# A conditioned convolution and gated-MLP block on one Trainium2 core: the MLP's transposes go to two PSUM tiles, GpSimd joins in normalizing and modulating, and the written-out order is new

## The chip, the cores and the metric

The kernel runs on one core of one Trainium2 chip. The core has a matrix engine (TensorE, "PE" in the profile; its weight loads are "PEld"), three elementwise engines (VectorE "DVE", ScalarE "ACT", GpSimd "POOL") and SyncE ("SP"), which here only starts DMA transfers. ACT starts some transfers too, in its own instruction stream. Every engine executes its instructions in the order in which they were written; between engines there are semaphores. The metric is the device time of one execution in microseconds (us), smaller is better, as the median of several executions.

## What is computed

The reference, cut to what matters (S = 2048 positions, D = 640 channels, 864 gate columns):

```
def A(q, k, v, shift_k, ssm_k, ssm_D):
    k_shift = sum over t of k_pad[:, t:t+S] * shift_k[:, 3-t]        # 4 taps
    kv = k_shift * v
    y = irfft(rfft(kv padded to 2S) * rfft(ssm_k padded to 2S))[:S]  # long convolution
    return q * (y + kv * ssm_D)

def B(x, w_in, w_sp, b_sp, w_out):
    z = gelu(x @ w_in)
    z1 = z[..., :864]
    z2 = layernorm(z[..., 864:])
    g = w_sp @ z2 + b_sp[:, None]
    return (z1 * g) @ w_out

sa, ca, ga, sb, cb, gb = split6(silu(c) @ w_mod)
x = A_q
h = layernorm(x) * (1 + ca) + sa
x = x + ga * A(h, A_k, A_v, ...)
h = layernorm(x) * (1 + cb) + sb
x = x + gb * B(h, ...)
```

All arrays are bf16.

## The kernel before

The 2048 positions are 16 tiles n = 0..15 of 128 rows, in four groups g = 0..3 of four tiles. The 640 channels are five units u = 0..4 of 128. All work up to the mixing matrix `w_sp` is put into a plan: `op(engines, kind, fn, r, w, new, n)` records an operation, the engines that may run it (P TensorE, A ScalarE, D VectorE, G GpSimd, S SyncE), what it reads and writes. The order in which all 1032 operations are issued, and the engine of each, stands written out in `ORDER` (line 40): `A147` means operation 147 on ScalarE. `Plan.run` (L112) only checks that an entry's engine is allowed and its inputs come earlier, and issues. An engine therefore works through its own entries strictly in that order; one that waits holds up everything behind it on its engine.

The stages, with the kinds of operations (the string in `op`) that the text uses:

- **Tables and the short convolution, to about 27 us.** `f1c` (L291) and `msin` (L340) are sines on ACT, after `silut` (L747), the warm-up that makes ACT load its first function table; `f1m` (L292), `msub`, `turns` build tables on DVE. `load_X` (L372) brings ssm_k in as tile X; for u = 0 it comes in two halves of 256 KB, and `addD` (L392) adds ssm_D to it on DVE. `ld1` (L738) loads three small vectors: shift_k (`skr`), ssm_D (`Dr`), c (`cr`). `turn1` turns them on PE, `skc` copies shift_k's columns, `diag` (L530, L528 on ACT) makes diagonal matrices of them, `taps` (L546) convolves k on PE and `tv` (L545) multiplies by v on DVE. `kvw` (L551) writes kv to a scratch in HBM, and `load_X` reads it back as XU0..XU4 in the layout for the transform.
- **The long convolution, about 27 to 121 us.** Per unit: stage 1 of the transform of ssm_k and of kv (`s1` on PE, `s1c` copies on ACT or DVE), stage 2 (`fwd` on PE; `khc` copies the kernel's spectrum on ACT), the product of the spectra (`prod`, L454, DVE), its sum into W (`csum`, L468, POOL or DVE), the inverse (`inv` on PE, `zc` copies to Z on ACT or DVE), a DMA transpose of Z to ZT (`zt`, L675), the last stage (`y` on PE, `ym`, L668, on DVE) and the residual (`res`, L688, DVE or POOL). In between run the first layernorm: statistics `ln1`, `rstd1` on POOL, normalizing `xn` (L598 on ACT, L600 otherwise, 128x640 a tile), and the modulation vectors: `ldw` (L610) loads a sixth of w_mod (800 KB) into the one buffer `wm`, `modr` multiplies; `ghm` (L651) applies them in two passes on POOL or DVE.
- **The turn into the MLP, about 121 to 140 us.** Unit 4 is turned on PE (`zfl`, L709; copies `zk`), `yl` is its last stage, `yml` (L730), `res` and the statistics `ln2` (L694), `ag2` (L813), `rstd2` (L184, L185 on POOL), `nmr2` (L817) follow. `zx` normalizes a tile of 128x640 (L827 on ACT, L829 otherwise). For group 0, in two pieces p of two tiles, `hfl` transposes on PE (L841) and `hmod` (L851 on ACT, L853 on DVE) multiplies by 1 + cb and adds sb while it copies from PSUM. For the groups 1 to 3 one DMA transpose a group (`turn`, L871) does the transposing and `hmod2` (L877 on ACT, L879 otherwise, 128x512) modulates in place.
- **The first MLP product, about 133.5 to 193.5 us.** `zz` is five matmuls of 128x432; 64 of them fill PE. Each is followed by `gelu` (L902, ACT), those of z2 by statistics (`stz`, `agz`, `rstdz`, `nmrz`) and `zn`, the normalization of 128x864 (L923 on ACT, L925 on DVE). `gelut` (L776) is a gelu of one column that makes ACT load the gelu table; before, it stands at the very end of ACT's entries.
- **Mixing and projection, 193.5 us to the end** (L964, L985), written as plain loops that the change does not touch.

`fill` operations (L931) are dummy matmuls on PE, `FILLS` gives how many each has. Tiles come from rings of buffers: `SLOTS` names how many buffers a tag has (PSUM tags s1 1, of two banks; sm, pu, pz 2 each, of one bank); a tile's first writer waits until the buffer's last tile is done with. Where two engines read the same PSUM tile, the framework lets them do so only one after the other: an instruction of one engine waits on a semaphore for the last instruction of the other. Transfers signal through eight semaphores that are handed out in turn, so a transfer waits until the one eight places before it, whoever issued it, has landed. 

Of the kernel before, what the change touches and what calls it, by code (L numbers as in the profile page):

```python
# [15 lines left out]
P = 128  # L16
# [8 lines left out]
NU = 5  # L25
# [8 lines left out]
FILLS = (4, 5, 1, 4, 3, )  # L34
# [6 lines left out]
D0 D100 D13 D14 A1 D15 G5 A2 A82 G101 D102 D103 S19 S21 D115 D116 A4 A16 D17 D6 D104 P1027 P7 A10 A23 P1028 P8 S83 A11  # L41
D86 A106 D109 P24 D110 P1029 P145 A105 A118 A117 A111 A147 D25 A146 D87 P148 A149 S20 A150 D121 D122 S523 D18 D119 P26
P151 S22 D27 S88 D153 P154 D155 A123 A124 G125 A120 P30 P28 A112 D31 G113 D114 D29 A152 A156 P165 A166 P163 A164 D127
A33 P139 D140 G126 P161 S32 A162 D90 G107 P133 P171 A172 P142 S34 D134 G135 P227 A228 P169 A170 D108 P136 G36 P157
A158 D143 G144 P229 A230 P167 D527 D528 G48 D529 D530 P37 S35 D38 A137 S84 A168 P159 P231 A160 P41 A232 D42 S3 P173
A175 D174 P176 D177 A178 G141 P39 D40 S85 P179 D181 S524 P182 A180 A183 A184 P43 D44 A531 A532 P185 D186 P233 G60 P9
A12 A533 P201 S46 S47 D202 P195 D196 P191 D192 G187 A234 P55 D56 P217 D218 A534 G188 P53 S45 G138 P189 A190 P211 D212
G197 G198 P199 A200 D54 P205 D206 G213 G214 D535 P49 P221 G207 G208 D222 P203 S526 A542 P51 S89 P251 D252 A204 P237
A543 P209 D52 S525 D538 A238 D210 P247 A248 D50 P257 A258 P215 D216 P241 P245 G130 G131 G72 A242 A246 P253 P193 D539
G536 D537 S565 P566 P249 A254 A544 A250 P568 P255 A256 D194 P235 D540 S91 D93 D549 D541 A236 P239 A240 S57 G223 G224  # L50
P225 P301 D302 A567 P243 A244 P259 D260 P219 D220 P303 P291 D292 S570 S58 A545 D546 P265 D266 A304 D550 A569 A226 P573
S92 P307 A308 P571 G261 G262 P263 A264 S59 P275 D276 P305 A306 P293 A294 G547 D548 D574 A557 P285 D286 G287 P325 A326
D558 D572 P267 D559 P309 A310 D551 D552 G707 D288 P269 D270 P327 A328 P65 D66 A561 G649 P315 A316 P329 A330 D562 P63
D64 D591 P295 P313 S575 P576 D577 A268 S94 D96 D296 A314 A128 D129 G271 P331 P289 A332 A560 S70 P61 G272 D62 P273 A274
G612 P375 A376 P333 D563 A290 G297 D298 P319 D553 A320 A554 P67 D595 D334 P377 A378 P299 D592 G596 P578 P323 A324 A555
A556 D68 D564 D579 D597 P349 D350 P73 P379 A380 G335 G336 G616 P343 A300 D344 D593 P77 G655 P337 P311 P321 A312 D598
S71 D78 A322 P381 D74 A382 A338 P369 D370 G594 P277 A278 D650 S599 P600 D601 G345 G346 P317 P279 D280 G371 A318 G372
P79 P347 A348 G618 P365 P351 A352 D80 G281 D282 P602 P383 G614 A384 S69 D366 S95 P399 A400 P359 G613 P387 A388 P373
P401 G656 A402 D603 P604 D653 P283 A284 A374 D360 P353 D605 P606 P403 A404 D361 G362 P395 D354 D607 P75 S97 D99 A396
D672 P397 A398 G676 G355 G356 P405 A406 G617 P385 D673 P339 D340 A386 P367 A368 S580 P449 G619 A450 D76 P413 D414 G615  # L60
P407 P363 P453 A454 G608 D408 S620 G409 A364 D410 G713 P341 P393 A394 P621 A342 P451 G654 P389 D622 G674 P623 D624
P439 P411 A390 A452 D440 P357 A358 P625 D626 P391 A392 P427 D428 A412 P455 G708 P627 P417 G429 S81 S98 A456 P415 A416
P473 A474 D418 G419 G420 P433 P457 A458 D430 D434 P431 D651 P479 G435 A480 P471 A472 D628 P443 D444 P475 A476 D629
P421 A432 P423 D424 P461 A462 P477 A478 D632 S657 P581 A582 G436 G652 P658 D659 G445 G446 P463 P481 D482 A464 A422
P437 A438 G675 G670 G671 P660 D661 P467 A468 G677 D633 P447 A448 P497 D498 G483 G484 P441 P662 D663 P517 D518 D630
G634 A442 P425 A426 P465 A466 P664 D665 G519 P459 A460 P507 P485 D508 P501 G520 D502 A486 P499 S583 A500 P469 A470
G609 P521 D637 A522 P513 P487 P584 D666 G509 G510 P511 A512 G503 A585 G504 D514 G714 S678 D488 P491 D492 G493 P515
A516 D494 P505 A506 P679 D680 P489 A490 G709 D636 S586 P681 D682 D635 P495 P683 D684 A496 P719 G610 G711 D720 P721
A722 P685 D686 G702 D687 D691 P717 P715 D716 A718 D689 P587 A588 D688 S753 D631 P723 D724 S754 D725 D726 P746 D727
D755 G667 D756 D728 D729 D747 G757 D758 P732 P589 D731 D690 D759 A760 D730 D768 D767 D692 P1030 P1031 P761 D762 D766  # L70
A764 A765 D763 P739 P789 P779 D693 G769 D770 A772 A771 G710 D733 D734 D736 D695 D738 D735 D638 A780 G712 P786 A787
A790 D696 P773 A775 D829 D737 G639 D831 A777 A778 P809 A810 G644 D694 D832 P811 A812 D830 P813 A814 D776 D774 D697
G668 D700 G833 D834 D835 A838 A837 D836 D669 S839 D740 D642 D741 D742 D744 D641 D703 D705 P815 A816 D745 D611 D645
A590 P793 A794 D748 D752 D743 P782 A783 P796 P819 A820 D841 A797 D798 P817 A818 P807 A808 D844 D842 A843 D640 D701
D643 D698 D898 D699 A840 P803 A804 D784 P800 A801 P821 A822 D895 D896 D897 G899 P845 A846 D847 D900 D901 D903 P862
A863 P885 P848 A886 D904 D802 A849 D850 A902 S905 P873 A874 P875 A876 P852 A853 P869 A870 D647 D805 D854 P866 A867
D648 P879 D750 A880 P855 A856 A910 D871 P859 A860 P881 A908 D788 D704 P883 A884 D646 A882 D751 P887 D962 D907 P877
A878 D909 D906 P951 P925 D706 D964 A952 P911 A888 A926 P932 P914 D749 D961 A933 P945 D963 G965 D966 D967 A912 A915
A946 D970 D968 P928 A929 D969 S971 D975 P947 D973 D974 A972 P921 A922 D976 D851 D934 P935 A936 D868 D872 D861 D864
P1001 A948 P977 A978 P984 A985 D806 D781 A1002 P987 A988 P939 D913 P1017 A1018 A940 D937 P1015 D857 A1016 P1019 D865  # L80
D795 D916 D858 A1020 D989 P998 G889 D890 A892 D1003 P994 D799 A999 A995 D785 A894 D986 D791 D792 G823 D824 P980 D1000
D1004 D828 A981 D979 P943 A944 P941 A942 D930 D982 D983 A825 P991 A992 D996 P1011 P918 A919 P1009 D927 D993 D997 D917
A1012 D931 D920 D923 D924 A827 D938 D893 D891 P1007 P1005 A1010 A1008 D990 G955 A826 D956 D958 A959 G1021 D1022 A1026
A1023 P953 A954 D960 P1013 A1014 A132 P949 A950 A1006 D1024 D957 D1025
# [39 lines left out]
def kernel(  # L124
# [26 lines left out]
    ND = D // P  # L151
# [52 lines left out]
    with ExitStack() as actx:  # L204
# [25 lines left out]
        def new(name, tag, shape, dtype=BF16, pool=None):  # L230
            if pool is None:
                pool = psA if tag in PSUM_TAGS else bigp if tag == "big" else span if tag in ("X1", "Z") else apool
            tl[name] = pool.tile(shape, dtype, tag=tag, bufs=SLOTS[tag], name=tag)
            return tl[name]
# [360 lines left out]
        def xn(n):  # L595
            def fn(e):
                if e is nc.scalar:
                    e.activation(gh[:, n, :], xt[:, n, :], ACT.Identity, bias=nmr1[:, n:n + 1], scale=rstd1[:, n:n + 1])  # L598
                else:
                    e.tensor_scalar(gh[:, n, :], xt[:, n, :], mv1[:, n, 0:1], rstd1[:, n:n + 1],  # L600
                                    op0=ALU.subtract, op1=ALU.mult)
            op("DA", "xn", fn, r=[("xt", (u, n)) for u in range(NU)] + [("mv1", n), ("rs1", n // 8)],
               w=[("gh", (u, n // TB)) for u in range(NU)])
# [207 lines left out]
        def norm_piece(g, p, ns, xn2):  # L811
# [7 lines left out]
            for i, n in enumerate(ns):  # L819
# [10 lines left out]
                op("DA", "zx", norm, r=[("mv2", n), ("rs2", (g, p)), ("nm2", (g, p))] + [("xt", (u, n)) for u in range(NU)] + ([] if first else [(xn2, "new")]),  # L830
                   w=[(xn2, n % TB)] + ([(xn2, "new")] if first else []), new=[(xn2, "Z")] if first else [])

        def flip_piece(g, p, ns, xn2, hT):
            k, i0 = len(ns), ns[0] % TB
            pt = "ft%d_%d" % (g, p)

            def flips(e):
                p_ = new(pt, "s1", [P, ND, k, P])
                for dt in range(ND):
                    for i in range(k):  # L840
                        e.transpose(p_[:, dt, i, :], tl[xn2][:, i0 + i, dt * P:(dt + 1) * P], ident[:])  # L841
            op("P", "hfl", flips, r=["ident"] + [(xn2, i0 + i) for i in range(k)], w=[pt], new=[(pt, "s1")], n=ND * k)
            for dt in range(ND):
                first = dt == 0 and p == 0

                def modulate(e, dt=dt, first=first):
                    if first:
                        new(hT, "Z", [P, ND, TC])
                    dst, src = tl[hT][:, dt, i0 * P:(i0 + k) * P], tl[pt][:, dt].rearrange("p a b -> p (a b)")
# [4 lines left out]
                op("AD", "hmod", modulate, r=[pt, "sb", "cb"] + ([] if first else [(hT, "new")]),  # L854
# [3 lines left out]
        def z_group(g):  # L858
# [9 lines left out]
            if g >= PE_GROUPS:  # L868
# [4 lines left out]
                for dt in range(ND):  # L873
# [6 lines left out]
                    op("DA", "hmod2", modulate, r=["sb", "cb"], w=[(hT, (dt, 0))])  # L880
# [159 lines left out]
```

## Time and profile before

| | us |
|---|---|
| median of 3 runs (lowest, highest) | 324.43 (323.75, 324.55) |
| the profiled execution | 323.44 |
| span of its profile | 321.7 |
| TensorE busy in the span | 306.5 (95%) |
| VectorE / ScalarE / GpSimd busy | 209.4 / 154.7 / 104.1 |
| granted TensorE clock, all slices | 0.9 or more of full speed; mean 1.00 |

How the page is read: an engine's busy time is the union of its instructions' spans; matmuls are pipelined, so the recorded length of one is longer than its place in the stream. "idle before ... <-X" says how long the engine had stood still before an instruction and whose end released it. The span leaves out the 1.74 us that lie around it in the execution.

### The profile page before, as it was taken

Reading aid. Unit: us, or ns where it says so; the run is one execution under the profiler, and the core shown is the slowest. Engines: PE = TensorE matmul, PEld = TensorE weight load, DVE = VectorE, ACT = ScalarE, POOL = GpSimd, SP = SyncE. Lnnn points to the kernel's source line nnn. Section 1 sums busy time; section 2 is a strip of 40 time slices with the busy share of each in tenths; the row PEclk is TensorE's granted clock in tenths of the full one; section 3 lists DMA queues with packets and bytes.
Section 4 is the critical chain, followed back from the end, with each engine's and each line's share of the span. In section 5 each row is a group of like instructions: output and inputs, shape, how many; then the busy total and the mean of one; then the engine's idle time right before and its main releaser. Section 6 shows DMA issues by size and latency. Waiting matters only on the chain.

```text
span 321.7 us, 6384 instructions
## 1 busy us (share of the span) xinstructions
PE 306.5 (95%) x2566; PEld 203.3 (63%) x2573; DVE 209.4 (65%) x450; ACT 154.7 (48%) x275; POOL 104.1 (32%) x130
## 2 busy tenths in 40 slices
PE   7898899999999998789999999999999999999996
PEld 2575688678898897445555555555555555555554
DVE  7999999899999899778837674442222222233233
ACT  5899899896988653597766785000000000000001
POOL 2366634778999987720010230000000000000000
PEclk9999999999999999999999999999999999999999
DMA  8999979997876397003439203998656555522221
GB/s 156 273 246 256 294 189 236 217 226 164 205 182 133 104 226 285 2 10 73 84 65 170 45 0 70 230 216 123 154 124 116 114 114 116 114 51 49 49 51 61
DMA packets 127025, 45.00 MB, mean 140 GB/s; under 512 B 116143, under 2 KB 126228, under 8 KB 126996
## 3 DMA queue, kind: packets, MB, share of 16 engines
q1 hardware_dynamic: 125562, 44.02, 61.6%
q10 hardware_dynamic: 1434, 0.57, 0.7%
q8 instruction: 20, 0.33, 0.5%
q14 instruction: 9, 0.07, 0.1%
HBM read 16.11 MB, written 5.24 MB: 66 GB/s over the span
## 4 chain that ended last, share of the span: by engine, by line
PE 74%; DMA 9%; DVE 8%; ACT 6%; issue 1%; POOL 1%; POOLq 0%; DVEq 0%; ACTq 0%; SPq 0%
PE ps L964 28%; PE pu L237 14%; PE pz L237 13%; PE po L985 9%; PE sm L237 5%; DMA wm<-in_w_mod_dram 4%; PE s L237 3%; DMA ZT<-Z 3%; DVE Tf L454 2%; ACT X L240 1%; DMA X<-kv_scr 1%; DMA kv_scr<-big 1%; ACT M L340 1%; DVE X L240 1%; ACT Z L851 1%
## 5 line engine op out<-in xcount | busy, mean ns | idle before, releaser
L964 PE MATMUL ps<-X,wT 128*128 128x432 bf16 x512 | 95.9, 346 | 0.2 <-ACT X L923 0.2
L964 PEld LDWEIGHTS <-wT 128*128 128x128 bf16 x512 | 50.0, 98 | 42.6 <-issue 0.5
L977 ACT COPY uT<-pt 128x896 bf16<-128x896 bf16 x1 | 0.9, 905 | 116.9 <-PE pt L976 116.9
L237 PEld LDWEIGHTS <-Z 128*128 128x128 bf16 x320 | 31.0, 98 | 29.9 <-DVE Z L853 3.2
L237 PE MATMUL pu<-X,M 128*128 128x128 bf16 (+1 forms) x480 | 45.3, 237 | 2.5 <-DVE Tf L454 1.2
L237 PEld LDWEIGHTS <-M 128*128 128x128 bf16 x480 | 37.1, 98 | 7.9 <-issue 2.9
L967 DVE SCALAR_TENSOR_TENSOR u<-ps,bcol,G 128x432 bf16<-128x432 f32 x18 | 12.0, 668 | 42.2 <-PE ps L964 42.2
L468 POOL TENSOR_TENSOR W<-Tf 128x256 bf16<-128x256 f32 x43 | 32.9, 783 | 16.7 <-DVE Tf L454 15.9
L237 PE MATMUL pz<-big,Z 128*128 128x432 bf16 x160 | 33.1, 346 | 1.5 <-DVE Z L853 1.5
L237 PE MATMUL pu<-big,Z 128*128 128x432 bf16 x160 | 32.8, 346 | 0.9 <-DVE Z L853 0.9
L985 PE MATMUL po<-w_o,uT 128*128 128x320 bf16 (+2 forms) x231 | 33.2, 295 | 0.1
L240 ACT CAST X<-s 128x1024 bf16<-128x1024 f32 x30 | 30.6, 1020 | 4.1 <-PE s L237 4.1
L454 DVE TENSOR_TENSOR Tf<-pu,KH 128x1024 f32<-128x1024 f32 x25 | 30.2, 1216 | 1.5 <-ACT KH L240 0.6
L985 PEld LDWEIGHTS <-uT 128*128 128x128 bf16 (+1 forms) x231 | 22.2, 98 | 9.9 <-issue 0.2
L967 DVE SCALAR_TENSOR_TENSOR u<-ps,bcol,M 128x432 bf16<-128x432 f32 x14 | 9.3, 667 | 28.7 <-PE ps L964 28.7
L237 PEld LDWEIGHTS <-G 128*128 128x128 bf16 x330 | 25.2, 98 | 2.5
L240 ACT CAST KH<-pu 128x512 bf16<-128x512 f32 x40 | 23.2, 596 | 4.5 <-PE pu L237 3.7
L240 ACT CAST Z<-pz 128x512 bf16<-128x512 f32 x36 | 20.7, 592 | 8.6 <-PE pz L237 8.1
L987 DVE TENSOR_TENSOR ot<-po,xt 128x320 bf16<-128x320 f32 (+1 forms) x33 | 15.9, 482 | 12.6 <-PE po L985 12.6
L237 PEld LDWEIGHTS <-X 128*128 128x128 bf16 x288 | 17.8, 97 | 6.0 <-issue 2.0
L237 PE MATMUL sm<-big,dg 128*128 128x512 bf16 (+3 forms) x73 | 19.7, 379 | 0.4
L237 PE MATMUL s<-F1bd,X 128*128 128x256 bf16 x128 | 19.2, 273 | 0.7 <-DVE X L240 0.5
(148 smaller groups left out, 421.0 us busy)
## 6 DMA issues: line engine op xcount, KB each, us to landing
wm<-in_w_mod_dram SPq DMA_DIRECT2D x6, 800.0 KB, 5.4
xt<-in_A_q_dram SPq DMA_DIRECT2D x4, 640.0 KB, 5.2
out_dram<-ot SPq DMA_DIRECT2D x15, 160.0 KB, 2.3
big<-in_B_w_in_dram SPq DMA_DIRECT2D x2, 1080.0 KB
X<-in_A_ssm_k_dram SPq DMA_DIRECT2D x4, 512.0 KB, 6.3
kv_scr<-big SPq DMA_DIRECT2D x4, 512.0 KB, 3.2
X<-kv_scr SPq DMA_DIRECT2D x4, 512.0 KB, 4.5
w_o<-in_B_w_out_dram SPq DMA_DIRECT2D x6, 160.0 KB, 3.0
```

Source lines behind the costliest of these rows:

```text
L237: nc.tensor.matmul(o, lhsT=w, rhs=x, start=start, stop=stop)
L240: (e.copy if e is nc.scalar else e.tensor_copy)(dst, src)
L340: op("A", "msin", lambda e, h=h, o=o: e.activation(M2[:, o, ks, 0:QH], tl[a][:, h], ACT.Sin, scale=-TWO_PI, bias=mturn[:, h * NCH + i:h * ...
L454: e.tensor_tensor(T_[:], (tl[pu] if src is None else tl[src])[:, :, :, None, :].to_broadcast(shape), tl[KH][:, :, None, :, :].to_broadcast ...
L468: e.tensor_tensor(tl[W][:, :, o, :], T_[:, :, 0, o, :], T_[:, :, 1, 1 - o, :], op=ALU.add if o else ALU.subtract)
L851: e.activation(dst, src, ACT.Identity, bias=sb_col[:, dt:dt + 1], scale=cb1_col[:, dt:dt + 1])
L964: nc.tensor.matmul(ps[:, :FC], lhsT=wTs[t][:, s_, :], rhs=tl["z2_%d" % (s_ // TB)][:, s_ % TB, fc * FC:(fc + 1) * FC], start=(s_ == 0), st ...
L967: nc.vector.scalar_tensor_tensor(u[:, sl], ps[:, :FC], bcol[:, t:t + 1], z1[t][:, sl], op0=ALU.add, op1=ALU.mult)
L977: nc.scalar.copy(uTs[t][:], pt[:])
L985: nc.tensor.matmul(ps[:, :hi - lo], lhsT=uTs[t][:fsz[ft], ft, :], rhs=w_o[:fsz[ft], ft, lo:hi], start=(ft == 0), stop=(ft == NFT - 1))
L987: nc.vector.tensor_tensor(ot[:, lo:hi], ps[:, :hi - lo], xt[:, t, lo:hi], op=ALU.add)
```

## The change

`flip_piece` makes two PSUM tiles of a piece in place of one: channels 0 to 2 in tag s1, which DVE alone reads, and channels 3 and 4 in tag sm, which ACT alone reads. `xn`, `zx` and `hmod2` may now run on GpSimd ("DAG" for "DA"). `FILLS` has four entries with 15 dummy matmuls, before five with 17. `ORDER` is new from the first entry to the last.

```diff
-FILLS = (4, 5, 1, 4, 3, )
+FILLS = (7, 2, 3, 3, )
 ...
-            op("DA", "xn", fn, r=[("xt", (u, n)) for u in range(NU)] + [("mv1", n), ("rs1", n // 8)],
+            op("DAG", "xn", fn, r=[("xt", (u, n)) for u in range(NU)] + [("mv1", n), ("rs1", n // 8)],
 ...
-                op("DA", "zx", norm, r=[("mv2", n), ("rs2", (g, p)), ("nm2", (g, p))] + ...
+                op("DAG", "zx", norm, r=[("mv2", n), ("rs2", (g, p)), ("nm2", (g, p))] + ...
 ...
-            pt = "ft%d_%d" % (g, p)
-            def flips(e):
-                p_ = new(pt, "s1", [P, ND, k, P])
-                for dt in range(ND):
-                    for i in range(k):
-                        e.transpose(p_[:, dt, i, :], tl[xn2][:, i0 + i, dt * P:(dt + 1) * P], ident[:])
-            op("P", "hfl", flips, ..., new=[(pt, "s1")], n=ND * k)
+            for dts, tag in ((range(0, 3), "s1"), (range(3, ND), "sm")):
+                def flips(e, dts=dts, tag=tag):
+                    p_ = new("ft%d_%d" % (p, dts[0]), tag, [P, len(dts), k, P])
+                    for j, dt in enumerate(dts):
+                        for i in range(k):
+                            e.transpose(p_[:, j, i, :], tl[xn2][:, i0 + i, dt * P:(dt + 1) * P], ident[:])
+                pt = "ft%d_%d" % (p, dts[0])
+                op("P", "hfl", flips, ..., new=[(pt, tag)], n=len(dts) * k)
 ...
-                op("AD", "hmod", modulate, ...
+                op("D" if dt < 3 else "A", "hmod", modulate, ...
 ...
-                    op("DA", "hmod2", modulate, r=["sb", "cb"], w=[(hT, (dt, 0))])
+                    op("DAG", "hmod2", modulate, r=["sb", "cb"], w=[(hT, (dt, 0))])
```

What the new list does with the engines (operations before, and after):

| kind | before | after |
|---|---|---|
| xn, 16 | 10 DVE, 6 ACT | 9 POOL, 4 DVE, 3 ACT |
| zx, 16 | 10 DVE, 6 ACT | 7 POOL, 5 DVE, 4 ACT |
| hmod2, 15 | 10 DVE, 5 ACT | 7 POOL, 3 DVE, 5 ACT |
| hmod, 10 | 5 DVE, 5 ACT | 6 DVE, 4 ACT |
| ghm, 40 | 29 POOL, 11 DVE | 23 POOL, 17 DVE |
| zn, 16 | 8 DVE, 8 ACT | 11 DVE, 5 ACT |
| csum, 50 | 43 POOL, 7 DVE | 42 POOL, 8 DVE |
| res, 21 | 9 POOL, 12 DVE | 11 POOL, 10 DVE |
| s1c, 48 / zc, 40 | 41 ACT, 7 DVE / 36 ACT, 4 DVE | 42 ACT, 6 DVE / 37 ACT, 3 DVE |
| msgn and mneg, 8 | 4 POOL, 3 DVE, 1 ACT | 7 POOL, 1 DVE |

And places in the order that the text comes back to:

- ACT begins with four transfers, the first half of X (256 KB), ssm_D, shift_k and c, and only then `silut` with its table. Before it began with shift_k, ssm_D, the first half of X, and SP brought c later. By the turn of the semaphores the load of shift_k now waits until the first half of X has landed; before, the load of X waited for shift_k.
- `diag` for channels 0..127 moves from ACT to DVE and stands there behind `f1m`, the index bits, an `msub` and the first `addD`. SP loads the second X (XK1) one place earlier, and DVE's `addD` of it stands ahead of `tv` 3 and 2.
- One `s1` of XK1 (0.44 us of PE) is moved ahead of the first `s1` of XU0. Otherwise PE's entries up to the MLP stand within a few places of where they were.
- `gelut` moves from the end of ACT's entries to the convolution of unit 2.
- The load of w_mod's last sixth moves from SP (behind the fourth use of `wm`) to ACT, behind the last `zc` and ahead of the `zk`; on PE the first `modr` of it moves from ahead of the `yl` to behind three of them.
- In the turn, ACT and POOL each normalize one tile of group 0's first piece and of its second (before ACT and DVE one each, then ACT two).

## The prediction, made before the changed kernel was run

> **What bounds the kernel now.** I read the busy times first, then the stretches between the stages' borders, then the timeline where TensorE (PE) stood still.
>
> ```profile
> PE 306.5 (95%) x2566; PEld 203.3 (63%) x2573; DVE 209.4 (65%) x450; ACT 154.7 (48%) x275; POOL 104.1 (32%) x130
> ...
> 27.00:62.00 35.00, 32.11 (x336) 26.09 (x336) 34.43 (x58) 32.47 (x64) 19.80 (x26) 1.00 0.99 243
> 62.00:96.00 34.00, 33.45 (x403) 28.56 (x407) 31.70 (x48) 28.64 (x45) 29.52 (x30) 1.00 0.89 196
> ...
> 128.30:133.50 5.20, 3.56 (x52) 2.11 (x49) 3.64 (x14) 1.94 (x3) 3.48 (x5) 1.00 0.02 3
> 133.50:140.50 7.00, 6.04 (x40) 3.33 (x41) 5.22 (x19) 6.59 (x12) 5.05 (x6) 1.00 0.00 0
> 140.50:193.50 53.00, 53.00 (x290) 28.29 (x291) 38.43 (x117) 38.80 (x71) 7.58 (x12) 1.00 0.37 68
> 193.50:196.10 2.60, 2.38 (x15) 1.17 (x12) 1.87 (x9) 2.16 (x3) 0.00 (x0) 1.00 0.01 3
> ```
>
> The columns of a stretch are its length and the busy us of PE, PEld, DVE, ACT and POOL, then the granted clock and the DMA. PE is the bound nearly throughout, at full clock: from 140.5 to 193.5 us it is never idle, and what follows 196.1 the change does not touch. So nothing that is taken off DVE or ACT behind 140.5 us is worth anything. What can be won lies where PE stands: the turn into the MLP, 128.3 to 140.5 us, and small waits up to 62 us, where DVE is busy 34.43 of 35 us: there DVE is a second bound. The other lines are of the turn:
>
> ```profile
> 131.99 1.02 ACT L851 ACTIVATE Z<-s,sb_col,cb_col 128x256 bf16<-128x256 bf16 x2 [1.90 <-DVE Z L853]
> 133.04 0.41 DVE L853 TENSOR_SCALAR Z<-s,cb_col,sb_col 128x256 bf16<-128x256 bf16 x1 [1.23 <-ACT Z L851]
> 133.51 2.30 PEld L237 LDWEIGHTS <-Z 128*128 128x128 bf16 x14 [1.80 <-DVE Z L853]
> ...
> 135.63 1.28 ACT L902 ACT_TABLE_LOAD   x1
> ...
> 139.70 0.73 DVE L853 TENSOR_SCALAR Z<-s,cb_col,sb_col 128x256 bf16<-128x256 bf16 x2 [1.68 <-ACT Z L851]
> 140.48 0.48 PEld L237 LDWEIGHTS <-Z 128*128 128x128 bf16 x4 [1.38 <-DVE Z L853]
> ```
>
> The five modulations of one PSUM tile run in turns, DVE, ACT, DVE, and PE waits for the last, twice. Between the two, ACT loads the gelu table. And the start:
>
> ```profile
> 0.72 0.56 ACTq L738 DMA_DIRECT2D KH<-in_A_shift_k_dram  x1
> 2.17 0.43 ACTq L382 DMA_DIRECT2D X<-in_A_ssm_k_dram  x1
> 2.63 1.28 ACT L747 ACT_TABLE_LOAD   x1 [2.63 <-DMA KH<-in_A_shift_k_dram]
> 5.65 0.42 DVE L292 TENSOR_TENSOR F1bd<-f1c,gmask 128x256 bf16<-128x256 f32 x1
> ...
> X<-in_A_ssm_k_dram SPq DMA_DIRECT2D x1, 256.0 KB, 4.7
> X<-kv_scr SPq DMA_DIRECT2D x2, 256.0 KB, 4.1
> ```
>
> ACT's table load stands behind its transfers, and the third of those waited for the landing of the first. The last number of a transfer is its us to landing.
>
> **Part 1, two PSUM tiles, first piece.** The transposes end at 130.87 us; the modulations take until 133.45 (2 on DVE, 2 on ACT, 1 on DVE) and the first `zz` starts at 133.51. Now DVE does three at its pitch, 0.33 + 0.33 + 0.41 = 1.07 us, and ACT two, 0.46 + 0.57 = 1.03, at the same time; with the 0.22 us from PE's end to DVE's start they are done 1.3 us after the transposes, before 2.58. That is 1.2 us, after a rounding down for ACT, which reads the later of the two tiles and copies gb first (2 x 0.42). It counts in full only if the transposes start no later than at 130.28. What leads to them: `yl` starts when the last `zk` is done, which doesn't move; then the same `yml`, `res`, `ln2`, `ag2`, `rstd2`, `nmr2`, and ACT's `zx` (0.92) in place of DVE's and ACT's, to about 130.2, equal. POOL's `zx` starts with `rstd2`'s end, at 128.94, as it needs no `nmr2`.
>
> **Part 2, second piece.** PE loses 1.1 us at 139.5 to 140.48, since ACT does two `zx`, the table (1.28) and three `gelu` before the second piece's modulations (138.17 to 139.66), and DVE's last two wait for ACT's (1.68). Now POOL does one `zx`, DVE's wait is gone, and `gelut` loads the table in the convolution, where ACT has room (28.64 of 34 us busy from 62 to 96). By the rows DVE reaches its three at about 137.6 and PE needs them at 139.3. I take the whole 1.1. What is late next is group 1, whose `hmod2` ended at 149.66, for a PE that needed it at 149.62. It stays hidden: `rstd2` of it can start with the last `ag2`, about 137.7, POOL's, ACT's and DVE's `zx` end near 140 (before 143.2), the transpose lands 4.9 us later, and POOL does two `hmod2` by 146.6; PE comes there at 147.5. With a slower POOL, part of this 1.1 goes. Bounds for both parts: -2.4 to 0.
>
> **Part 3, GpSimd's rates.** The trace has no POOL normalization. Nearest rows: a tensor-scalar of 128x512 with one column operand takes 702 ns, one of 128x1024 with constants 1043, a 128x512 tensor-tensor 1188 to 1199. For 128x640 with two columns I take 0.85 us (from the first, plus 128 elements at the slope to the second and one more column), bounds 0.72 and 1.5 (the tensor-tensor by 640/512). Nine `xn` are 7.7 us of POOL, paid for by six `ghm` (6 x 1.18 = 7.1) that go to DVE (6 x 0.5 = 3.0) while DVE drops six `xn` (3.1): even. Per stage it is not even: in the order, DVE gets 0.6 us less up to 55 us, then 2.3 less, then 2.6 more. PE's waits in 27 to 121 us (about 5 us in 15 places) were mostly for DVE. I take -0.6, bounds -2.5 to +2.5: the list is new everywhere and I can't follow each wait.
>
> The Trainium skill speaks against this part: Perfetto Trace Analysis, Optimizing Scalar/DVE Operations, says that GpSimd shares a read port with the vector engine under an exclusive lock, so moving work between those two may not help. The row for it: the same DVE normalization takes 510 ns as `xn`, beside a busy POOL, and 438 as `zx`, mostly beside a quiet one, 72 ns dearer and far from a POOL instruction's length. By the rule, with each of 23 moved instructions stopping DVE for its whole 0.85 us, up to 20 us of DVE would be lost and the time would rise. By the row alone the loss of DVE is 23 x 0.07 = 1.7 us, mostly behind 128 us, where DVE has room (38.43 of 53 us busy).
>
> **Part 4, the start.** ACT issues the first half of X at 0.72; shift_k waits for its landing. The other half of that load took 4.7 us, the 256 KB read-backs 4.1; I take 4.1, as little else is in flight: landing at 4.8 (bounds 4.1, by the 3.4 of the 256 KB write, and 5.4). Then shift_k (0.56), c (0.53), the table (1.28), `silut` (0.20), `f1c` (0.31): 7.7. DVE's `f1m` waits for that, where before it ran at 5.65: 2.0 us lost, and behind it stand the index bits, `msub`, `addD`, `diag` and all `tv`. DVE drops 1.5 us of other work up to the last `tv` of kv0 and gains 0.7, so `kvw`, the read-back and the first `s1` of XU0 are 1.3 us later. In that time PE does the `s1` of XK1 that was moved ahead (0.44). Net +0.9; bounds 0 and +2.2, the upper with the late landing and a wait for XK1, whose `addD` DVE now has ahead of two `tv`.
>
> **Part 5, at no cost.** The 800 KB of w_mod are issued at about 121.7 from ACT; the six took 4.8 to 6.1 us, so they land by 127.8, and the moved `modr` is due at 127.7. The cover is the chain to `zx`: PE waits for it till 130.28 anyway and needs 2.0 us for `modr` twice and the fill, so nothing is lost up to 128.3; the w_in load beside it could make it 1.5 later, the upper bound. At the end, the 0.22 us wait at 196.10 goes, since DVE takes three of ACT's `zn` (0.49 for 1.1 us): -0.2, bounds -0.2 and +1.
>
> **Sum.** -1.2 - 1.1 - 0.6 + 0.9 + 0 - 0.2 = -2.2 us. The profiled execution's 323.44 (span 321.70 and 1.74 around it) becomes 321.2. The median of the runs shown lies 0.99 above the profiled one, so I predict 322.2.
>
> **Rivals.** *The start eats the gain*: the late landing and the wait for XK1 (+2.2), with a DVE that is full from 27 to 62 us and hands the delay on, so that part 3 gives nothing: 324.43 - 2.5 + 2.2 = 324.1. For it: 34.43 of 35 us; against it: DVE gets less work there. Chance 0.2. *GpSimd becomes the bound*, the slower case: four `xn` in a row stand on POOL ahead of unit 1's first `csum`, four more ahead of a later one, and a late sum stops PE's `inv` and everything behind. It decides from about 1.1 us an `xn`: at 1.5 the eight are 8 x 0.65 = 5.2 us later, of which I leave out 1 us of slack in each run: +3.2, and group 1's 1.1 is lost too: 322.2 + 4.3 = 326.5. For it: POOL is busy 29.52 of 34 us from 62 on; against it: only 19.80 of 35 before. Chance 0.22. *More than I see*: the start costs nothing and part 3 reaches -2: 322.2 - 0.9 - 1.4 = 319.9. Chance 0.15. My forecast has 0.40; 0.03 is left for other mishaps.
>
> **From these the numbers.** A measurement here tells some 0.3% (1 us) from no change. Faster: 0.36 of my 0.40, the 0.15 and 0.02 of the first rival, 0.53. Same: 0.03 and 0.14 of the first rival, 0.17. Slower: the rest, 0.30. The forecast's own range is 320.5 to 323.8; taking in half of both outer cases gives 319.6 to 326.0.
>
> **What would show it.** In the changed profile: DVE's and ACT's modulations (L853 and L851) side by side and no wait of PE for them near 139 us; no table load among the gelus; ACT's first table load at 5 to 7 us and DVE idle before `f1m`; the first `s1` of XU0 0.5 to 1.5 us later than 22.44; POOL's 128x640 at 0.72 to 1.1 us. I am wrong if PE's idle time between 27 and 121 us grows by over 2 us, if `modr` waits for w_mod past 128.5, or if POOL's normalizations take over 1.1 us.

## The result, and the profile after

| | before | after |
|---|---|---|
| median of 4 runs each, us (lowest, highest) | 324.09 (323.04, 324.55) | 344.69 (343.37, 346.09) |
| ratio, 95% interval | | 1.064 (1.058 to 1.070) |
| profiled execution / span, us | 323.44 / 321.7 | 343.37 / 341.2 |
| GpSimd busy, us | 104.1 | 147.8 |
| granted TensorE clock, mean | 1.00 | 0.979 |

The kernel became 20.6 us slower, where I had forecast 2.2 us faster. (One run further down, of mfront_xn with 327.56 us, was in a slower state of the chip and is left out of the medians.) From the page of the changed kernel, its engines, the chain that ended last, and the group of GpSimd's first normalization:

```profile
PE 311.2 (91%) x2571; PEld 205.2 (60%) x2571; DVE 210.7 (62%) x437; ACT 147.5 (43%) x263; POOL 147.8 (43%) x152
...
PE 59%; POOL 17%; DVE 10%; DMA 9%; issue 3%; ACT 1%; ACTq 0%; POOLq 0%; DVEq 0%
...
L600 POOL TENSOR_SCALAR gh<-xt,mv,rstd 128x640 bf16<-128x640 bf16 x9 | 23.1, 2577 | 0.0
```

A normalization takes GpSimd 2577 ns. I had taken 850, with 1500 as the upper bound. POOL is busy only 43% of the span, and still 17% of the chain. What that does is in the timeline of the changed kernel:

```profile
48.69 10.07 POOL L600 TENSOR_SCALAR gh<-xt,mv,rstd 128x640 bf16<-128x640 bf16 x4
58.73 1.40 POOL L468 TENSOR_TENSOR W<-Tf 128x256 bf16<-128x256 f32 x2
...
60.19 1.01 PE L237 MATMUL pz<-W,G 128*128 128x256 bf16 x6 [5.08 <-POOL W L468]
...
67.74 10.20 POOL L600 TENSOR_SCALAR gh<-xt,mv,rstd 128x640 bf16<-128x640 bf16 x4
```

Four `xn` in a row hold POOL from 48.69 to 58.76 us. The two sums (L468) behind them are late, and TensorE, whose `inv` reads them, stands for 5.08 us. The second row of four, from 67.74 us on, stops TensorE by another way:

```profile
77.98 0.94 DVE L651 TENSOR_TENSOR gh<-gh,gca_bf 128x512 bf16<-128x512 bf16 x1 [4.89 <-POOL gh L600]
...
82.14 1.01 PE L237 MATMUL pu<-X,M 128*128 128x256 bf16 x6 [4.38 <-DVE Tf L454]
```

Here DVE stands 4.89 us for the last of the four, in front of a `ghm` (L651). The product of the spectra (`prod`, L454) is behind that in DVE's list, and TensorE waits 4.38 us for it. The stretches of the changed kernel (length, busy us of PE, PEld, DVE, ACT and POOL, granted clock, DMA) show a second cost:

```profile
44.00:54.00 10.00, 10.00 (x110) 8.67 (x108) 9.30 (x21) 9.97 (x20) 8.72 (x7) 1.00 1.03 201
54.00:62.00 8.00, 2.92 (x27) 2.46 (x25) 4.73 (x10) 2.54 (x4) 7.83 (x6) 0.72 1.12 243
62.00:70.00 8.00, 8.00 (x70) 5.99 (x68) 5.15 (x7) 6.17 (x9) 6.30 (x6) 0.85 1.19 216
...
76.00:84.00 8.00, 3.62 (x28) 2.65 (x26) 6.02 (x10) 1.54 (x3) 7.92 (x6) 0.84 0.01 2
```

While POOL works without a pause, DVE and ACT run dry with TensorE, and the granted clock of the stretches is 0.72, 0.85 and 0.84, where the kernel before has 1.00: TensorE also does the next work more slowly. The same stretches before:

```profile
54.00:62.00 8.00, 7.26 (x78) 5.79 (x76) 7.72 (x15) 7.71 (x12) 4.58 (x5) 1.00 1.06 231
76.00:84.00 8.00, 7.95 (x114) 7.06 (x112) 7.71 (x12) 5.65 (x10) 7.99 (x9) 1.00 1.03 236
```

Behind the turn it is the groups' normalizations, again in the timeline of the changed kernel:

```profile
156.82 2.67 POOL L829 TENSOR_SCALAR Z<-xt,mv,rstd 128x640 bf16<-128x640 bf16 x1
...
159.52 3.11 SPq L871 DMA_TRANSPOSE Z<-Z  x1
...
164.55 1.63 POOL L879 TENSOR_SCALAR Z<-Z,cb_col,sb_col 128x512 bf16<-128x512 bf16 x2 [3.93 <-DMA Z<-Z]
```

That is group 1: the transpose starts when POOL's `zx` ends, POOL's two `hmod2` follow the landing, and TensorE loses 1.3 us there. With groups 2 (two `zx` on POOL, 5.0 us) and 3 (5.2 us) its delay grows by 5.3 us in all.

To place every loss I line the kernels up by TensorE's own work: each step of the plan counts with its usual pitch (`s1`, `fwd` and a two-tile `inv` 0.44 us, `taps` and a four-tile `inv` 0.87, `zz` 0.91, and so on), dummy matmuls count nothing, and the start of a step minus the work ahead of it is its delay. The change of that delay against the kernel before, in us, from the profiled executions; madd and mfront are two of the experiments below:

| TensorE work done, us (time in the kernel before) | after | madd | mfront |
|---|---|---|---|
| 20 (30.6, unit 0) | +3.7 | +5.2 | +2.1 |
| 40 (52.3, unit 1) | +2.2 | +4.7 | +0.6 |
| 60 (73.5, unit 2) | +13.9 | +4.8 | +0.9 |
| 100 (115.5, unit 4) | +14.4 | +4.4 | +0.9 |
| 118 (140.5, behind the turn) | +14.7 | +2.3 | -1.2 |
| 170 (192.6, last `zz`) | +19.9 | +2.2 | -1.3 |

The spans differ by 19.5, 1.8 and -1.5 us, so hardly anything happens behind the last `zz`. The column "after" has three losses: 3.7 us in the start, 11.6 between work 40 and 60, 5.3 behind the turn.

### The profile page after: what moved, and what is told of

Same layout as the page of the kernel before. It is cut to its first block, busy times and chain, and to the rows that moved or that the text cites. A ratio compares the mean times of both kernels' runs of the same rounds, so it can differ in the third digit from the quotient of the medians.

```text
span 341.2 us, 6386 instructions
## 1 busy us (share of the span) xinstructions
PE 311.2 (91%) x2571; PEld 205.2 (60%) x2571; DVE 210.7 (62%) x437; ACT 147.5 (43%) x263; POOL 147.8 (43%) x152
## 4 chain that ended last, share of the span: by engine, by line
PE 59%; POOL 17%; DVE 10%; DMA 9%; issue 3%; ACT 1%; ACTq 0%; POOLq 0%; DVEq 0%
PE ps L964 27%; PE pu L237 9%; PE po L985 9%; PE pz L237 8%; POOL gh L600 5%; DMA ZT<-Z 5%; PE sm L237 4%; POOL Z L829 4%; DMA Z<-Z 3%; POOL rstd L185 2%; POOL W L468 2%; DVE Tf L454 1%; DMA big<-in_A_k_dram 1%; POOL gh L651 1%; POOL Z L879 1%
## 5 line engine op out<-in xcount | busy, mean ns | idle before, releaser
L237 PE MATMUL pu<-X,M 128*128 128x128 bf16 (+1 forms) x480 | 46.0, 238 | 5.7 <-DVE Tf L454 5.3
L468 POOL TENSOR_TENSOR W<-Tf 128x256 bf16<-128x256 f32 x42 | 31.0, 755 | 11.3 <-DVE Tf L454 9.3
L454 DVE TENSOR_TENSOR Tf<-pu,KH 128x1024 f32<-128x1024 f32 x25 | 30.2, 1218 | 5.2 <-PE pu L237 5.1
L237 PEld LDWEIGHTS <-G 128*128 128x128 bf16 x330 | 26.0, 101 | 7.9 <-issue 5.4
L240 ACT CAST Z<-pz 128x512 bf16<-128x512 f32 x37 | 21.7, 592 | 17.1 <-PE pz L237 17.0
L237 PE MATMUL sm<-big,dg 128*128 128x512 bf16 (+1 forms) x80 | 22.6, 414 | 0.9 <-DVE big L545 0.9
L600 POOL TENSOR_SCALAR gh<-xt,mv,rstd 128x640 bf16<-128x640 bf16 x9 | 23.1, 2577 | 0.0
```

The source lines that it names most:

```text
L237: nc.tensor.matmul(o, lhsT=w, rhs=x, start=start, stop=stop)
L240: (e.copy if e is nc.scalar else e.tensor_copy)(dst, src)
L454: e.tensor_tensor(T_[:], (tl[pu] if src is None else tl[src])[:, :, :, None, :].to_broadcast(shape), tl[KH][:, :, None, :, :].to_broadcast ...
L468: e.tensor_tensor(tl[W][:, :, o, :], T_[:, :, 0, o, :], T_[:, :, 1, 1 - o, :], op=ALU.add if o else ALU.subtract)
```

## The experiments

The theory: GpSimd's rate for this instruction makes it the bound, and the rest of the change is worth about what was predicted. Rivals: the new list and its start cost the time; or the port that GpSimd shares with DVE stretches both. The times, each against runs of the kernel before on the same chip, whose median was 323.9 to 324.5 us (forms was run once):

| kernel | median us | ratio (95% interval) |
|---|---|---|
| forms | 324.68 | |
| madd | 324.13 | 1.001 (0.998 to 1.004) |
| xn_back | 333.49 | 1.027 (1.023 to 1.031) |
| all_back | 342.55 | 1.058 (1.054 to 1.063) |
| mfront | 321.40 | 0.992 (0.988 to 0.995) |
| mtable | 324.79 | 1.003 (1.000 to 1.005) |
| mone | 326.34 | 1.009 (1.006 to 1.012) |
| bturn | 330.47 | 1.021 (1.019 to 1.024) |
| bturn2 | 322.82 | 0.998 (0.996 to 0.999) |
| mfront2 | 321.48 | 0.992 (0.990 to 0.994) |
| mfront_xn | 322.84 | 0.996 (0.993 to 0.998) |
| mfront3 | 323.19 | 0.995 (0.993 to 0.997) |

### What makes GpSimd's 2577 ns (forms)

```diff
+    def probe(k):           # called behind mix(2) ... mix(13), with k = 0 ... 11
...
+        for rep in range(2):
+            if rep: nc.vector.memset(go[:], 0.5); c0 = go[:]
+            if k == 0: e.tensor_scalar(o, i, c0, c1, op0=ALU.subtract, op1=ALU.mult)
+            elif k == 1: e.tensor_scalar(o, i, c0, c1, op0=ALU.mult, op1=ALU.add)
...
+            if rep:
+                for _ in range(4):
+                    nc.vector.tensor_scalar(dve_out[:], xt[:, 0, :], pc[:, 0:1], pc[:, 1:2], op0=ALU.subtract, op1=ALU.mult)
```

> The kernel before with twelve forms of a GpSimd instruction on 128x640 (two of them 128x512) of scratch, put into the mixing stage behind 212 us, where GpSimd has no other work; each once with DVE left to its own work, and once with four normalizations of DVE (128x640, bf16) started at the same time. Theory 'its own rate': subtract-then-multiply with two columns takes about 2.5 us in both, as in the changed kernel. If the order of the operations makes the rate, multiply-then-add takes 0.8 to 1.1 us; if the width or the writing to another tile makes it, 2.5 us too. Rival 'the shared port': alone it takes 0.85 to 1.5 us, and over 2 us only beside DVE, and DVE's 436 ns grow by over 100 ns beside it. The time stays within 1% of the kernel before, as the scratch work lies beside the rest.

Its groups on GpSimd from 190 us on (busy us, mean ns, idle before). In the order of the lines: subtract then multiply, multiply then add, multiply alone, multiply by a column then add a constant, a tensor-tensor addition:

```profile
L1010 POOL TENSOR_SCALAR pool_out<-pool_in,go,pc 128x640 bf16<-128x640 bf16 x1 | 2.6, 2611 | 17.0 <-DVE go L1007 17.0
...
L1012 POOL TENSOR_SCALAR pool_out<-pool_in,pc 128x640 bf16<-128x640 bf16 x1 | 0.9, 875 | 0.1
...
L1018 POOL TENSOR_SCALAR pool_out<-pool_in,pc 128x640 bf16<-128x640 bf16 x1 | 1.9, 1887 | 0.1
...
L1020 POOL TENSOR_SCALAR pool_out<-pool_in,pc 128x640 bf16<-128x640 bf16 x1 | 0.8, 799 | 0.1
...
L1030 POOL TENSOR_TENSOR pool_out<-pool_in 128x640 bf16<-128x640 bf16 x2 | 2.5, 1252 | 0.2
```

It is the kind of operations, not the width, the columns or another target: subtract-then-multiply took 2499 to 2882 ns in its four runs, in place or not, with DVE's work beside it or not. Multiply-then-add took 875 and 914 ns, multiply twice 877 and 915, add-then-multiply 885 and 925. On 128x512 it is the same: 2078 and 2107 ns for subtract-then-multiply, 768 and 812 for multiply-then-add. One operation alone is slow too: 1887 to 2061 ns. The first theory holds; the shared port does not make GpSimd slow.

### The changed kernel with the quick form (madd)

```diff
+                elif e is nc.gpsimd:
+                    e.tensor_scalar(gh[:, n, :], xt[:, n, :], rstd1[:, n:n + 1], nmr1[:, n:n + 1],
+                                    op0=ALU.mult, op1=ALU.add)
                 else:
                     e.tensor_scalar(gh[:, n, :], xt[:, n, :], mv1[:, n, 0:1], rstd1[:, n:n + 1],
                                     op0=ALU.subtract, op1=ALU.mult)
```

`zx` likewise, with `rstd2` and `nmr2`. List and engines stay, so that madd tells GpSimd's rate from the list as the cause.

> The changed kernel, with GpSimd's sixteen normalizations written as x times rstd plus (-mean times rstd), as ACT does them, in place of subtract-then-multiply; list and engines stay. If the form makes the 2577 ns: 128x640 at 0.85 to 1.1 us and a time of 320 to 325 us. If GpSimd needs 2.5 us for two columns on 640 elements in any form: 343 to 346 us, as the changed kernel. If the new list or the start cost the time: 335 us or more, even where GpSimd's instruction gets short.

The two groups of normalizations on GpSimd in madd:

```profile
L600 POOL TENSOR_SCALAR gh<-xt,rstd,nmr 128x640 bf16<-128x640 bf16 x9 | 8.2, 921 | 0.8 <-ACT ga L639 0.8
L832 POOL TENSOR_SCALAR Z<-xt,rstd,nmr 128x640 bf16<-128x640 bf16 x7 | 6.6, 954 | 2.0 <-DVE nmr L820 1.2 <-ACT X L907 0.4 <-issue 0.4
```

921 and 954 ns, and 324.13 us: two operators written otherwise are worth 20.6 us. Both losses in the middle and behind the turn are gone (in the table, madd keeps its +4.7 from work 40 to 60 and gets no later behind 118; TensorE is busy 54.00 of the 54 us from 140 to 194). But with GpSimd at nearly the rate that I had assumed, the time is that of the kernel before and not 2.2 us less. (madd's profiled execution, 325.59 us, lies 1.5 above its median, so the table shows it later than its usual run.) A second term of the sum is wrong too: the start.

### The work given back to DVE and ACT (xn_back, all_back)

```diff
-D0 ... G553 ... G554 ... G549 ... G550
+D0 ... D553 ... A554 ... D549 ... D550
```

So for nine `xn` in xn_back, and in all_back also for seven `zx` and seven `hmod2`, at the same places of the list.

> The changed kernel with the nine xn of GpSimd given back to DVE (7) and ACT (2) at the same places of the list; zx and hmod2 stay on GpSimd. 'GpSimd became the bound': TensorE's two waits of 5.2 and 4.6 us near 54 and 77 us go, and what follows 140 us stays, so 331 to 335 us, with the clock at 1.0 in 54 to 84 us. 'The list costs it': over 338 us.

> The changed kernel with all xn, zx and hmod2 of GpSimd given back to DVE (21) and ACT (2) at the same places. 'GpSimd became the bound': 321 to 327 us, since the 6 to 8 us behind 140 us go too; DVE has 9.5 us more to do, some of it in the turn into the MLP. 'The list costs it': over 338 us; 'the start costs it': 327 to 335 us, with the loss ahead of 40 us.

xn_back: 333.49 us, as expected. From work 20 to 100 its delay grows by 4.2 us and madd's by 4.4: in these two executions it makes no difference whether the nine `xn` stand on GpSimd at the good rate or on DVE and ACT.

all_back is a miss: 342.55 us, nearly as slow as the changed kernel, though no normalization is left on GpSimd. Its waits of DVE and of TensorE:

```profile
DVE Z L893 <- DMA Z<-Z: 15.3, 3, 5.9
...
PE pu L251 <- DVE Z L893: 9.9, 3, 4.7
```

DVE stood 15.3 us in all, three times, in front of a `hmod2` (L893) whose transpose had not landed, with the statistics of the next groups behind it, and TensorE waited 9.9 us for it. In the changed kernel GpSimd stood 3.9 to 5.2 us at these places itself and DVE only 1.3, 3.9 and 1.3. So the experiment does not say what the seven `hmod2` and `zx` would cost on DVE; it says that a place in the list belongs to the engine for which it was chosen. That the list costs the time by itself, as all_back alone could be read, madd rules out: it has the changed kernel's list and takes 324.13 us.

### The start (mfront)

```diff
-D100 G5 D0 G101 S19 A82 D13 A2 D15 D14 G6 A1 P1029 P7 A3 D102
+D100 G5 D0 G101 S19 A1 A2 A82 D13 D15 D14 G6 P1029 P7 D102
...
-S84
+S84 S3
```

That is madd with ACT's transfers in the old order (shift_k, ssm_D, half of X) and c on SP.

> madd with the start of the kernel before on ACT's queue alone: shift_k, ssm_D, then the first half of X, and c issued later from SP; the rest of the new list stays. 'The start is the second cost': the table load at about 2.6 us, F1 at 5.7 in place of 7.5, TensorE 2.5 to 4 us earlier from 12 us on, and a time of 320 to 322 us. 'The delay is handed back later' (DVE or a transfer sets the pace anyway): 323.3 to 325 us.

321.40 us, 0.992 (0.988 to 0.995) of the kernel before and, with mfront2 below, the fastest of all; against madd the ratios differ by 0.009, about 3 us (plus or minus 1.4). ACT's table load starts at 2.18 us in mfront, and at 5.58 us in the changed kernel:

```profile
5.58 1.28 ACT L747 ACT_TABLE_LOAD   x1 [5.58 <-DMA big<-in_A_k_dram]
...
7.32 0.43 DVE L292 TENSOR_TENSOR F1bd<-f1c,gmask 128x256 bf16<-128x256 f32 x1 [1.85 <-ACT f1c L247]
...
9.14 0.39 PE L237 MATMUL pz<-F1bd,X 128*128 128x256 bf16 x2 [1.85 <-DVE X L392]
```

DVE waits 1.85 us and starts `f1m` at 7.32 us, before at 5.65. I had f1c done at 7.7; it was done at 7.29. The delay of that link was right. What I did not follow is TensorE behind it: its first product of X comes at 9.14 in place of 7.50 us, and the first `s1` of XU0 at 25.67 in place of 22.43, 2.8 us later at equal work, where I had 0.9 net.

### The early gelu table and the two PSUM tiles (mtable, mone)

```diff
-... A338 P369 D370 G346 G614 S599 P600 A132 P351
+... A338 P369 D370 G346 G614 S599 P600 P351
...
+... A132 D1026
```

> madd with the early load of the gelu table put back to the end of the list, so that the first gelu loads the table between the two pieces of the turn. 'Part 2 is worth about 1 us': TensorE waits for ACT's two modulations of the second piece, 324.6 to 325.4 us. 'ACT has room there': 324.1 us, no change.

```diff
-            for dts, tag in ((range(0, 3), "s1"), (range(3, ND), "sm")):
+            for dts in (range(0, 3), range(3, ND)):
...
-                    p_ = new("ft%d_%d" % (p, dts[0]), tag, [P, len(dts), k, P])
+                    p_ = tl[pt] if dts[0] else new(pt, "s1", [P, ND, k, P])
```

In mone's list the two halves of a piece's transposes also follow each other.

> madd with one PSUM tile for each piece in place of two (both halves of the transposes write it, DVE still reads three fifths, ACT two). 'The readers of one tile go one after the other': the second reader starts only after the first reader's three, each piece 1.0 to 1.2 us later, 325.2 to 326.5 us. 'The order of the list alone does it': 324.1 us, no change.

mtable's ratio is 0.002 above madd's, within the error of both. In the traces TensorE loses 0.5 us between work 112 and 118 in mtable and 0.1 in madd: the early table is worth some 0.4 us here, not 1.

mone costs 0.008 more than madd, about 2.6 us (plus or minus 1.4). First mtable's timeline, with two tiles (the line of DVE, then of ACT), then mone's, with one:

```profile
134.20 1.05 DVE L872 TENSOR_SCALAR Z<-s,cb_col,sb_col 128x256 bf16<-128x256 bf16 x3 [0.21 <-ACT gb_bf L661]
134.41 1.02 ACT L870 ACTIVATE Z<-sm,sb_col,cb_col 128x256 bf16<-128x256 bf16 x2 [0.27 <-ACT gb_bf L661]
```

```profile
134.23 1.05 DVE L872 TENSOR_SCALAR Z<-s,cb_col,sb_col 128x256 bf16<-128x256 bf16 x3 [0.43 <-issue]
...
135.45 1.02 ACT L870 ACTIVATE Z<-s,sb_col,cb_col 128x256 bf16<-128x256 bf16 x2 [1.50 <-DVE Z L872]
...
136.52 0.54 PE L251 MATMUL pu<-big,Z 128*128 128x432 bf16 x2 [0.83 <-ACT Z L870]
```

With two tiles the engines read side by side; with one, ACT starts after DVE's third, and TensorE waits for it.

### The turn alone, in the old list (bturn, bturn2)

Into the kernel before, with its own list: `flip_piece` of the changed kernel, three `hmod` on DVE and two on ACT a piece, and `gelut` early. bturn2 moves one entry more:

```diff
-D735 D638 A782 G712 P788
+D735 D638 A782 G712 D740 P788
```

> The kernel before with its own list, with the two PSUM tiles for each piece, DVE for three modulations and ACT for two, and the early load of the gelu table; nothing on GpSimd, the start as it was. By parts 1 and 2 of the prediction: TensorE's waits of 1.9 and 1.1 us near 131 and 138 us go, 321.8 to 323 us. Rival 'what is late next takes it': 323.8 to 324.8 us, with a new wait at group 1's first product near 147 us.

> bturn with one step of the list moved: DVE's multiplication of the last unit's group 2 (yml) before the second piece's modulations, since its PSUM tile held the slot that the second piece's second tile needs (TensorE waited 5.5 us for it at 136.2 us). 'Parts 1 and 2 are worth what was predicted, where the slot is free': 321.5 to 323 us, TensorE without a wait of over 0.5 us from 130 to 150 us. 'What is late next takes it': 323.5 us or more.

bturn was 6.5 us slower, which neither theory had. From its timeline:

```profile
140.97 0.68 DVE L744 TENSOR_TENSOR gh<-gh,sm 128x512 bf16<-128x512 bf16 x1
...
141.71 0.61 PE L854 MATMUL sm<-ident,Z 128*128 128x128 bf16 x4 [5.54 <-DVE gh L744]
```

The second tile is in tag sm, and its buffer was still held by the sums of the last unit's group 2, whose reader (`yml`, L744) stood far behind in DVE's list. With that `yml` moved ahead (D740), bturn2 takes 322.82 us, 0.8 us less than before. That is within the expected 321.5 to 323, but not free of waits: before the product at 132.26 us TensorE stood 1.16 us for a buffer of sm that ACT was still reading, and before the one at 140.42 us 0.53 for ACT's two modulations of the second piece, which came behind other work. In a list made for one tile, parts 1 and 2 bring 0.8 us (0.3 to 1.4) of the 2.3.

### Beyond mfront (mfront2, mfront_xn, mfront3)

```diff
-FILLS = (7, 2, 3, 3, )
+FILLS = (7, 4, 3, 3, )
...
-D100 G5 D0 G101
+D0 D100 G5 G101
```

> mfront with the identity built first on DVE and two more filling products ahead of the first products of X, so that TensorE starts at 1.7 in place of 2.46 us and does not pause at 6.9 us. In mfront a pair of 256-column products takes 0.61 to 0.64 us from 7.2 to 9 us, where the kernel before has 0.38. 'TensorE's rate depends on how long it has been busy': 0.38 us from 7.5 or 8 us on, and 319.8 to 321 us. 'It is the clock of the stage, or DVE sets the pace there': 321.2 to 322.2 us.

> mfront with the nine xn of GpSimd back on DVE (7) and ACT (2), at the same places; GpSimd keeps its seven zx, as multiply-then-add, and its seven hmod2. 'At the good rate the nine xn on GpSimd are worth what part 3 said': 0.6 us slower, 321.7 to 322.5 us. 'They are worth nothing either way': 321.0 to 321.8 us. 'They are worth 2.5 us, the bound': 323.5 to 324.5 us.

> mfront2 with the products of w_mod's third part (modr of mod0) four TensorE steps later, and DVE's two rows and one ghm that hang on them later too. mfront2 started 2.4 us earlier and gave it back near 58 to 62 us, where TensorE waited 1.9 us for that part's landing and then ran at a lower rate. 'The transfer is the next bound there and can be hidden': 319 to 320.5 us. 'The gain goes at the next place (the turn at 128 to 132 us)': 320.8 to 321.6 us.

mfront2 starts TensorE at 1.65 us and does the first products of X at 0.38 us a pair, so that at work 20 to 40 it is 2.4 us ahead of mfront, and the time is the same, 321.48 us. Before 60.47 us it waits 1.94 us for the landing of w_mod's third part, and the ten products behind that take 2.46 in place of 1.53 us: two thirds of the lead go to this wait and to the lower clock behind it (0.66 granted from 60 to 65 us, 1.00 in mfront), the rest in the turn. mfront3 hides most of that wait and is no faster (323.19 us); it loses 1.1 us between work 20 and 30, and 2.5 us at the turn's start (work 110 to 112), as mfront2 does, where mfront loses 0.9. There too the clock differs: from 128 to 134 us 0.72 is granted in mfront2 and in mfront3, 1.00 in mfront. Why it fell in the one and not in the other was not tried. mfront_xn is mfront with the nine `xn` on DVE and ACT: 0.004 (plus or minus 0.004) above mfront by the times, while from work 20 to 100 the delays grow alike (3.9 and 4.0 us). So the nine `xn` on GpSimd bring nothing that the traces show, and the times leave 0 to 2.6 us open.

## Why the prediction was wrong

- **Part 3, GpSimd's rates, is the step that failed.** It took 0.85 us for a normalization, "from the first, plus 128 elements at the slope to the second and one more column", bounds 0.72 and 1.5. The rows that it leaned on were all of a quick kind: both its tensor-scalars (L345 and L367) multiply twice. That the two operations themselves could change the rate threefold no row showed, so the bounds should have been left open above. Measured: 2.58 us. The rival that named the mechanism, "GpSimd becomes the bound", was right in place: two runs of four `xn`. The first stopped PE's `inv` by a late `csum`, as it said; the second came by DVE, whose `ghm` waited for an `xn` with a `prod` behind it. Its own formula with the measured rate gives 8 x (2.58 - 0.85) - 2 = 11.8 us; TensorE lost 11.6 between work 40 and 60. That they agree so well is luck in part: the two waits are 5.08 and 4.38 us, and the lower clock behind them, which adds to the loss, is not in the formula. What it left out are the groups behind the turn: it counted 1.1 us for group 1, and 5.3 went with groups 1 to 3.
- **Part 4, the start: the mechanism was right, the term too small.** +0.9 net, at most +2.2; in madd TensorE is 5.2 us behind at work 20 (3.3 to 5.2 in the profiled executions of the six kernels with this start), and 3 of that goes with ACT's order alone (mfront). The lateness of `f1m`, 2.0 us, was nearly met (1.7). Missing were TensorE's own later start (2.46 for 1.64 us, since DVE builds the identity behind three other instructions), its low rate in the products that follow (in madd from 9.35 to 14.6 us each takes about twice its later time), and that nothing handed the delay back before the turn: from work 40 to 100 madd stays 4.4 to 4.8 us late.
- **Part 3's gain of 0.6 us** did not come: madd is as late at work 100 as at work 40, and the traces show no gain of the nine `xn`.
- **Parts 1 and 2, -2.3 us, held** where GpSimd is quick: from work 100 to 118 the kernel before loses 6.6 us, madd 4.5, so 2.1 less, and mfront is 2.1 better too. mfront2 and mfront3, with the lower clock there, gain less. The modulations lie side by side, and no table load stands among the gelus. In the changed kernel itself the slow `zx` took it all: 6.8 us lost there, as the prediction said ("With a slower POOL, part of this 1.1 goes").
- **Part 5** was small: TensorE waits 0.33 us for w_mod's last part in the changed kernel and not visibly in madd, whose 1.42 us before 66.47 us are for the third part; the bound was 1.5. **The tail** gained some 0.4 us in madd (2.2 us late at the last `zz`, 1.8 in the span); -0.2 was taken.
- So the sum would have missed with the right rate too: -2.1 for the turn and about +4.4 for the start make madd's +1.8 of span, where -2.2 was forecast. By the medians, where madd is level with the kernel before, it misses by 2.2 us, and the start comes to about 2 us in place of 0.9. "I am wrong if ... POOL's normalizations take over 1.1 us" was the sign that decided.

**The skill's rule.** The prediction set aside that GpSimd and DVE share a port under an exclusive lock, by a row that showed 72 ns. The forms kernel shows the lock: DVE's normalization takes 442 to 447 ns with GpSimd quiet, 887 to 947 ns where it starts beside a quick one of about 0.9 us, and 1255 to 1305 beside a tensor-tensor of 1250 to 1307 ns; it ends about 0.2 us after the other. From the timeline of forms, three of DVE's beside the tensor-tensors, and three with GpSimd quiet:

```profile
285.10 3.92 DVE L1035 TENSOR_SCALAR dve_out<-xt,pc 128x640 bf16<-128x640 bf16 x3
...
292.85 1.41 DVE L1035 TENSOR_SCALAR dve_out<-xt,pc 128x640 bf16<-128x640 bf16 x3
```

The Trainium skill says so (SBUF — State Buffer, Who interferes with whom: where VectorE's instruction uses both ports, the first to issue holds the shared pair for its whole length and the other fully blocks), and these rows agree. My 72 ns was an average over meetings and misses: before, eight of the ten `xn` on DVE took 435 to 457 ns, the others 659 and 933. But the lock was not what cost the time: beside the slow form on 128x640 DVE is held once, 880 ns, and its next two take 447 each inside the same GpSimd instruction, so there the measurement does not show a hold over its whole length. And madd keeps all GpSimd work, with the lock, at the time of the kernel before. On the rate itself page and measurement differ: the GPSIMD Engine Reference (Engine selection) calls one-input work on GpSimd roughly line-rate. That fits the 0.8 to 0.9 us of the quick forms, and not the 1.9 to 2.9 us of the others; the measurement decides.

## What to carry to other kernels

Before work is moved to GpSimd, time the very instruction there, with its operations and not only its shape: here subtract-then-multiply takes 2.6 us and the same normalization as multiply-then-add 0.9, and these two expressions are worth 20 us. A cost bounded by rows of other operations has no upper bound, and a queue of four such instructions ahead of a sum that TensorE needs multiplies the error by four. A list made for one assignment of engines does not carry to another: the same places on DVE made it stand for a transfer, and a second PSUM tile needs a buffer that the old list still held.

## What the runs showed of the hardware that I had not expected

- **GpSimd's tensor-scalar has two speeds**, by the operations: on 128x640 bf16, 0.80 to 0.93 us for multiply-add, multiply-multiply and add-multiply, 1.9 to 2.9 us for subtract-multiply and for one operation alone. Why was not tried.
- **TensorE's first products differ from run to run, with the clock.** mfront and mfront_xn have the same list up to the first `xn`, behind 40 us. In the profiled execution of mfront a pair of 256-column products takes 0.61 to 0.64 us from 7.2 to 8.9 us, and its delay at work 2 is 9.0 us; in that of mfront_xn it is 7.2. mfront2, with TensorE started 0.8 us earlier, has 0.38 us. The line is of mfront:

```profile
7.20 0.61 PE L251 MATMUL pz<-F1bd,X 128*128 128x256 bf16 x2 [0.31 <-DVE X L406]
```

  The stretches of mfront read 1.00 there all the same, but its trace holds no record of the granted clock before 11.34 us; the first one, of full clock, begins there, and at that point the 512-column products pass from 0.43 to 0.22 us apiece. The first record begins at 5.1 us in the kernel before, at 6.3 in mfront_xn and mfront2 and at 14.6 in madd, and in each the long products end there. This may be a part of why mfront's times lie between 319.48 and 322.49 us; executions without a profile do not show it.
- **A pause costs more than its length**: around the 5.08 us wait the granted clock was 0.72 in 54 to 62 us and 0.85 in 62 to 70. Taken finer, it is 0.50 from 57.6 to 64.3 us, though TensorE had gone on at 60.19: the six products there take 1.01 us, and six of the same kind 0.60 at 71.90, at full clock.
